# Another order of all operations in a gated recurrence with a highway layer

## The chip, the cores and the metric

The kernel runs on one core of a Trainium2 chip. The metric is the device time of one execution in microseconds (us). The core has five engines with an instruction queue each: TensorE (PE in the profile, its weight loads PEld), VectorE (DVE), ScalarE (ACT), GpSimd (POOL) and SyncE (SP), which here only issues the DMAs of the large tensors.

## The reference

The first stage is a gated linear recurrence over the tokens of four sequences, the second a highway layer on its result.

```python
# x, f_logit: (4, 6336, 256) float32; lower_bound: (256,)
sig = 1.0 / (1.0 + np.exp(-f_logit))
f = lower_bound + (1.0 - lower_bound) * sig
for t in range(6336):                       # h starts at 0 in each sequence
    h = f[:, t] * h + (1.0 - f[:, t]) * x[:, t]
    y[:, t] = h
# y as (25344, 256); w_h, w_t: (256, 256); b_t: (256,)
H = np.maximum(y @ w_h, 0.0)
T = 1.0 / (1.0 + np.exp(-(y @ w_t + b_t)))
out = T * H + (1.0 - T) * y
```

## The kernel before

The 25344 tokens are cut into 29 units: two of 2 blocks of 128 tokens, three of 4 blocks, 22 of 8 blocks (1024 tokens), one of 4 and one of 2. A unit goes through a fixed chain of operations, most of them once for each half (0 or 1) of the 256 channels:

| entry | engine | what it does |
|---|---|---|
| l, x | SP | load f_logit and x of the unit (up to 1 MB each) |
| u | ScalarE | sigmoid(-f_logit), both halves |
| b | GpSimd, or VectorE where marked v | product of u and x, one half |
| i | TensorE | transposes of u into PSUM, so that tokens lie along the free axis |
| f | ScalarE, or VectorE where marked v | the gate f from the transposed u |
| p | TensorE | transposes of b |
| s | VectorE | the scan: y = f * previous y + b along the tokens; it carries on from the unit before |
| z, g | TensorE | matmuls of y with w_t and with w_h |
| t | ScalarE | sigmoid of z |
| d | VectorE | the larger of g and a multiple of y, one half |
| e | GpSimd, or VectorE where marked v | product of d and t, cut into pieces of 256 to 2048 elements |
| o | TensorE | transposes d*t back and adds y, in PSUM |
| c | ScalarE, or VectorE where marked v | copies o to SBUF |
| w | SP | stores 4 blocks of the result (512 KB; single blocks in the last unit) |

An entry such as "e7.2v:1" names the operation, the unit (7), the half or piece (2), VectorE instead of the usual engine (v), and the buffer (1). The units 9 to 21 have one e for the whole unit (2048 elements); units 2 to 4 have two pieces, the other large ones three (1024, 512, 512). Besides these there are the entries of the start (dg, cb, cc, pc, pb, IW, WHa, WTa, wh, wt: constants and weights) and "k*n", n matmuls on zeros that only keep TensorE busy.

The order of the work is written out by hand as one string of 850 entries. A loop at the end takes the entries one by one and emits their instructions, and each engine's queue keeps that sequence (`pin`). So an instruction that has to wait also holds up all that follow it on its engine. The framework adds the waits for data and for the reuse of buffers: PSUM has two buffers a (one bank) for i and p, and three b (two banks) for z, g and o; SBUF has 6 of l and x, 4 of u and f, 8 of b and y, 5 of o.

Beside these waits there is one by hand. When GpSimd gets a product, it waits for the last VectorE product that stands ahead of it in the order, if no GpSimd product has waited for that one yet. There is no such wait in the other direction:

```python
    def shared(ins, gpsimd):
        if not gpsimd:
            held[:] = [ins]
        elif held:
            tc.add_manual_dep(ins.ins, held.pop().ins.name, ...)
```

The lines that the profile names: L268 is u, L276 b, L284 i, L293 and L295 f (VectorE, ScalarE), L304 p, L323 s, L335 and L115 z and g, L348 t, L352 d, L358 e, L380 and L381 o, L391 and L393 c (VectorE, ScalarE), L256 the loads, L397 the stores, L126 and L115 the matmuls on zeros.

Of the kernel before, what the change touches and what calls it, by code (L numbers as in the profile page):

```python
# [57 lines left out]
b6.0:5 f6.1:2 d4.0 k*3:1 p6.1:0 s6.1:4 i6.0:1 l8:2 u7:3 z5.1:1 g5.1:2 x8:2 b7.1:6 b7.0:7 f6.0:0 t4.0 t5.1:2 i7.1:1 p6.0:0
z5.0:0 f7.1:1 d5.1:2 t5.0 o3.0:1 g5.0:2 i7.0:1 c3.0:3 s6.0:5 e5.1v w1.0 l9:3 e4.0 x9:3 w0.0 e5.2v p7.1:0 l10:4 w2.0 d5.0 e5.0
g6.0:0 z6.1:1 z6.0:2 u8:0 f7.0:3 t6.1:1 i8.0:1 e4.1v b8.0:1 b8.1:0 s7.1:6 f8.0v:2 l11:5 w3.0 t6.0 x10:4 x11:5 u9:1 d6.0:0  # L60
i8.1:0 g6.1:1 p7.0:1 s7.0:7 o5.1:2 f8.1:0 c5.1:1 o5.0:0 i9.1:0 d6.1 e6.0 p8.1:1 c5.0:0 f9.1:1 e6.2 z7.0:2 t7.0:0 o4.0:0
p8.0:0 c4.0:2 u10:2 w5.1 b9.1:3 e6.1 l12:0 w4.0 l13:1 g7.1:1 s8.1:2 i9.0:1 g7.0:2 o6.0:0 s8.0:3 i10.1:0 f9.0:3 b9.0:2 x12:0
# [10 lines left out]
c11.0v:3 z13.1:0 f18.0:1 t13.1 g14.0:1 d14.0:1 i16.0:0 w11.0 b16.1:1 e13.0 p15.0:1 l20:2 f16.0:3 u17:2 z14.0:2 s15.0:6
o12.0:0 g14.1:1 i16.1:0 t14.0:2 b17.0:3 c12.0:0 x18:0 p15.1:1 o12.1:2 d14.1 s15.1:7 f16.1:0 w12.0 z14.1:1 c12.1:1 p16.0:0
i17.0:1 t14.1 g15.1:0 z15.0:2 w12.1 x19:1 s16.0:2 p16.1:0 f17.0:2 o13.0:1 d15.1:0 u19:3 t15.0:1 p17.0:1 o13.1:0 c13.0:2
c13.1:3 b17.1:2 e14.0 s16.1:3 z15.1:2 i17.1:0 g16.0:1 s17.0:0 g16.1:0 d16.0:2 t15.1 f17.1:3 x20:2 d16.1 u20:0 i18.1:1 z16.0:2
t16.0:0 p17.1:0 g15.0:1 z16.1:0 f18.1:0 w13.1 l21:4 b18.0:4 b18.1:5 t16.1 s17.1:1 w13.0 o14.0:2 d15.0 l22:3 i19.1:1 o14.1:0
c14.0:0 f19.1:2 z17.1:1 p18.0:0 e16.0v c14.1:1 b19.1:6 w14.0 b19.0:7 x21:3 e15.0v i19.0:1 t17.1:2 g17.0:2 z17.0:0 f19.0:3
o16.1:1 b20.0:0 s18.0:4 b20.1:1 t17.0 c16.1:3 p18.1:1 i20.0:0 f20.0:1 u21:2 d17.0:1 s18.1:5 g17.1:0 o16.0:2 d17.1 p19.1:0
w14.1 c16.0:2 z18.1:1 z18.0:0 p19.0:1 t18.1:0 e17.0 w16.1 o15.1:2 s19.1:2 l23:5 s19.0:3 x22:4 b21.0:3 i21.1:0 g18.1:1 t18.0  # L80
c15.1:0 g18.0:0 f21.1:0 d18.1:2 w15.1 u22:1 i20.1:1 f20.1:2 d18.0 b21.1:2 e18.0 p20.0:0 o15.0:2 z19.1:1 w16.0 o17.0:0 s20.0:6
p20.1:1 c15.0:1 b22.0:4 b22.1:5 g19.0:2 c17.0:3 t19.1:1 i21.0:0 f21.0:3 u23:3 x23:5 g19.1:0 s20.1:7 z20.0:1 p21.0:1 d19.0:0
t20.0:2 o17.1:2 w15.0 p21.1:0 d19.1 s21.0:0 o18.1:0 b23.1:6 s21.1:1 c17.1:0 z19.0:1 z20.1:2 i22.0:1 c18.1:2 t19.0 t20.1
g20.1:0 d20.1:1 f22.0:1 e19.0v l24:0 o18.0:1 w17.1 i22.1:0 g20.0:2 c18.0:1 f22.1:2 i23.1:1 z21.0:0 f23.1:3 d20.0 p22.0:0
o19.0:1 l28:1 x24:0 t21.0:0 w17.0 s22.0:4 p22.1:1 g21.1:2 o19.1:0 d21.1:2 s22.1:5 i23.0:0 c19.0:0 u24:0 f23.0:0 l25:2 w18.0
w19.0 z21.1:1 t21.1 b23.0:7 c19.1:3 g21.0:2 e20.0 i24.1:0 p23.1:1 d21.0 s23.1:2 z22.1:1 f24.1:1 b24.0:0 b24.1:1 e21.0 g22.0:0
z22.0:2 d22.0:0 p23.0:0 t22.1:1 u25:2 t22.0 w18.1 x25:1 w19.1 i24.0:1 o20.0:1 f24.0:2 c20.0:1 g22.1:0 s23.0:3 o20.1:2 i25.0:1
p24.0:0 d22.1 c20.1:0 o21.0:1 g23.0:0 u28:1 f25.0:3 e22.0 e22.1 e22.2 l26:4 c21.0:2 s24.0:6 d23.0:1 w20.0 z23.1:2 i28.1:1
p24.1:0 o21.1:1 f28.1:0 t23.1:2 s24.1:7 i28.0:1 c21.1:3 f28.0:2 g23.1:0 o22.0:2 x26:2 d23.1 u26:3 i25.1:1 b25.0:3 b25.1:2
e23.1 p25.0:0 c22.0:1 s25.0:0 f25.1:1 e23.2v z24.0:1 z24.1:0 g24.1:2 i26.1:0 p25.1:1 t24.0:0 f26.1:3 t24.1 d24.1:2 s25.1:1  # L90
z23.0:1 g24.0:2 w21.1 l27:3 i26.0:0 b26.0:4 b26.1:5 t23.0 o22.1:0 z25.1:1 p26.1:1 d24.0 e24.2v x27:3 u27:0 w22.0 w20.1 x28:4
g25.0:2 c22.1:3 e24.0 t25.1:1 b27.1:6 e24.1 e23.0v b27.0:7 b28.0:0 f26.0:1 s26.1:4 d25.0:0 w22.1 o23.1:0 z25.0:1 c23.1:1
# [345 lines left out]
```

## Time and profile before

| what | us |
|---|---|
| time, median of 3 runs | 206.16 (205.93 to 207.3) |
| span of the profiled execution | 204.7 |
| VectorE busy | 193.0 (162 instructions) |
| ScalarE busy | 193.1 (201) |
| TensorE busy | 191.6 (1826 matmuls) |
| GpSimd busy | 175.6 (98) |
| DMA | 78.68 MB, 384 GB/s over the span |

The profile gives one execution's span, from its first to its last instruction; it names no time of its own for that execution, which is therefore set beside the runs' median (1.46 more than the span). Busy time is the sum of an engine's instructions. A row of the timeline has the start, the time from there to the end of the last instruction of the row, engine and line, operation, output and inputs, shapes and count; in brackets stands the idle time ahead of it and what ended it. On an engine the next instruction mostly starts a little before the one ahead is reported as finished, so the time that an instruction takes up on its queue is read from one start to the next. A row that groups instructions has their count, then busy us and the mean ns of one, then the idle time before them.

### The profile page before, as it was taken

The page shows a single profiled execution, that of the slowest core. Times are in us where ns is not written, and L with a number is a line of the kernel's source. Part 1 is how long each engine was busy: PE and PEld are TensorE (multiplying, and loading weights), DVE is VectorE, ACT ScalarE, POOL GpSimd, SP SyncE. Part 2 cuts the span into 40 slices and gives each one's busy share as a digit, 9 for nine tenths or more (in the row PEclk, how much of TensorE's full clock was granted, in tenths as well). Part 3 has the DMA queues.
Part 4 walks back from the last instruction along what each step waited for, and adds up shares of the span by engine and source line. Part 5 has one row for each costly group of instructions (what it writes and reads, how often), then busy time and mean ns, then how long its engine had stood idle before and what let it go on. Part 6 is the DMA issues. An engine that isn't in the chain of part 4 may idle for free. (4 is left out here: it accounts for less than half of the span.)

```text
span 204.7 us, 4658 instructions
## 1 busy us (share of the span) xinstructions
PE 191.6 (94%) x1826; PEld 131.9 (64%) x1826; DVE 193.0 (94%) x162; ACT 193.1 (94%) x201; POOL 175.6 (86%) x98
## 2 busy tenths in 40 slices
...
GB/s 176 387 415 429 410 421 415 413 424 420 422 419 411 429 423 415 425 415 422 428 402 426 429 417 419 418 425 423 413 337 400 425 390 307 352 283 22 396 330 241
DMA packets 16413, 78.68 MB, mean 384 GB/s; under 512 B 1796, under 2 KB 2568, under 8 KB 10760
## 3 DMA queue, kind: packets, MB, share of 16 engines
...
q10 hardware_dynamic: 8, 0.00, 0.0%
...
## 5 line engine op out<-in xcount | busy, mean ns | idle before, releaser
L276 POOL TENSOR_TENSOR bv<-u,x 128x1024 bf16<-128x1024 f16 (+2 forms) x53 | 104.2, 1988 | 14.8 <-DVE d L358 5.7
L323 DVE TENSOR_TENSOR_SCAN y<-f,y,bT 128x1024 bf16<-128x1024 f16 (+5 forms) x56 | 106.9, 1925 | 0.2
L358 POOL TENSOR_TENSOR d<-d,t 128x512 bf16<-128x512 bf16 (+3 forms) x32 | 70.4, 2213 | 4.1 <-DVE d L358 1.8
L352 DVE SCALAR_TENSOR_TENSOR d<-y,ncc,g 128x1024 bf16<-128x1024 bf16 (+2 forms) x58 | 63.2, 1105 | 0.3 <-PE g L115 0.2
L348 ACT ACTIVATE t<-z,bt 128x1024 bf16<-128x1024 f32 (+2 forms) x58 | 62.4, 1112 | 0.8 <-PE z L115 0.8
L295 ACT ACTIVATE f<-uT,ncc 128x1024 f16<-128x1024 f16 (+2 forms) x55 | 60.8, 1120 | 0.8 <-DVE y L323 0.2
L393 ACT COPY o<-op 128x1024 f32<-128x1024 f32 (+2 forms) x53 | 52.8, 1036 | 1.9 <-ACT t L348 1.0
L268 ACT ACTIVATE u<-l 128x2048 f16<-128x2048 f32 (+2 forms) x29 | 51.5, 1776 | 2.5 <-DMA l<-in_f_logit_dram 2.5
L380 PE MATMUL op<-diag,y 128*128 128x128 f16 x396 | 49.7, 219 | 0.9 <-ACT t L348 0.4
L381 PE MATMUL op<-ident_b,d 128*128 128x128 bf16 x396 | 49.7, 219 | 0.8 <-POOL d L358 0.8
L381 PEld LDWEIGHTS <-d 128*128 128x128 bf16 x396 | 44.0, 113 | 4.8 <-POOL d L358 1.7
L380 PEld LDWEIGHTS <-y 128*128 128x128 bf16 x396 | 44.2, 113 | 2.3
L335 PE MATMUL z<-y,w_sb 128*128 128x512 bf16 (+1 forms) x116 | 40.0, 368 | 0.8 <-DVE d L352 0.3
L335 PE MATMUL g<-y,w_sb 128*128 128x512 bf16 (+1 forms) x116 | 40.3, 368 | 0.0
L304 PE MATMUL bT<-ident_f,bv 128*128 128x128 f32 x198 | 32.1, 278 | 2.9 <-DVE y L323 1.1
L115 PE MATMUL g<-y,w_sb 128*128 128x512 bf16 x88 | 33.3, 379 | 0.0
L115 PE MATMUL z<-y,w_sb 128*128 128x512 bf16 x88 | 33.3, 379 | 0.0
L284 PE MATMUL uT<-ident_h,u 128*128 128x128 f16 x396 | 31.4, 219 | 2.0 <-DVE y L323 1.1
L284 PEld LDWEIGHTS <-u 128*128 128x128 f16 x396 | 25.9, 98 | 11.1 <-issue 3.1
L335 PEld LDWEIGHTS <-w_sb 128*128 128x128 f16 x232 | 22.3, 98 | 15.7 <-ACT f L295 0.2
L304 PEld LDWEIGHTS bT<-ident_f,bv 128*128 128x128 f32 x198 | 22.1, 140 | 13.3 <-issue 4.7
L115 PEld LDWEIGHTS <-w_sb 128*128 128x128 f16 x176 | 17.2, 98 | 15.8 <-issue 1.7
...
## 6 DMA issues: line engine op xcount, KB each, us to landing
...
l<-in_f_logit_dram SPq DMA_DIRECT2D x22, 1024.0 KB, 14.0
...
```

What stands on the lines that cost most here:

```text
L115: return pe.add_instruction(mybir.InstMatmult(name=nc.get_next_instruction_name(), start_tensor_calc=start, stop_tensor_calc=stop, tile_si ...
L276: shared(pin(e.tensor_mul(bv[:, :nb // 2].rearrange("p k d j -> p k j d"), st[n]["u"][:, :nb, own].rearrange("p (k j) d -> p k j d", j=2), ...
L284: pin(nc.tensor.transpose(uT[:, j * P:(j + 1) * P], st[n]["u"][:, j, h * P:(h + 1) * P], ident_h))
L295: pin(nc.scalar.activation(to, of, AF.Identity, scale=ncc[:, h:h + 1], bias=1.0))
L304: pin(nc.tensor.transpose(words[:, k:k + g * (P - 1) + 1:g], pair, ident_f))
L323: pin(nc.vector.tensor_tensor_scan(y[:, c:e], st[n]["f", h][:, c:e], st[n]["bT", h][:, c:e], 0.0 if fresh else carry[h], op0=ALU.mult, op1 ...
L335: pin(nc.tensor.matmul(p[:, a:e], w, half(n, "y", ki)[:, a:e], start=ki == 0, stop=ki == NH - 1))
L348: pin(nc.scalar.activation(half(n, "t", m), st[n]["z", m][:, :tokens(n)], AF.Sigmoid, bias=bt[:, m:m + 1]))
L352: pin(nc.vector.scalar_tensor_tensor(half(n, "d", m), half(n, "y", m), ncc[:, m:m + 1], st[n]["g", m][:, :tokens(n)], op0=ALU.mult, op1=AL ...
L358: shared(pin(e.tensor_mul(st[n]["d"][:, a:c], st[n]["d"][:, a:c], st[n]["t"][:, a:c])), not eng)
L380: pin(nc.tensor.matmul(o, half(n, "y", h)[:, cols], diag[:, h], start=True, stop=False))
L381: pin(nc.tensor.matmul(o, half(n, "d", h)[:, cols], ident_b, start=False, stop=True))
```

## The change

Only the string of the order is changed: the same operations of the same units stand in another sequence, with other buffer numbers, and some go to another engine. On VectorE there are five f instead of three, 18 e instead of 22, two c instead of four, and the same number of b. The matmuls on zeros are 27 in both, at other places. The diff, cut to the start, the places around the VectorE products of units 3 to 11 and of 15 and 16, and the end:

```diff
     order = """
-k*3:a0 x0:0 pc:0 l0:0 l1:1 cc u0:0 k*3:1 pb:2 i0.0:1 k*4:0 dg wh u1:1 b0.1v:0 f0.0:0 b0.0v:1 i1.0:0 x1:1 l2:2 wt IW f1.0v:1 p0.0:1
-WHa cb i0.1:0 s0.0:0 f0.1:2 x2:2 b1.1v:2 b1.0v:3 k*2:0 i1.1:1 k*1:0 p0.1:0 f1.1:3 p1.0:1 s0.1:1 k*1:0 p1.1:0 l3:3 g0.0:0
-s1.0:2 g0.1:1 u2:2 s1.1:3 x3:3 k*1:2 i2.1:1 d0.1:0 l4:4 WTa d0.0 g1.0:2 i2.0:0 g1.1:1 z1.1:0 b2.1v:4 f2.1:0 d1.1:1 d1.0
-f2.0:2 p2.1:1 s2.1:4 b2.0:5 t1.1:0 z0.0:1 z0.1:0 z1.0:2 u3:3 x4:4 t0.1:1 t1.0 t0.0 l5:5 x5:5 p2.0:0 b3.1:6 i3.1:1 f3.1:1
-s2.0:5 e0.1v e0.0v e1.1v k*3:0 i3.0:0 g2.0:0 l6:0 u4:0 e1.0v x6:0 b3.0:7 z2.0:2 b4.0:1 f3.0:3 p3.1:1 t2.0:2 d2.0:2 g2.1:1
-i4.1:0 o0.0:0 z2.1:2 f4.1:0 s3.1:6 b4.1:0 d2.1 c0.0:0 t2.1 p3.0:1 i4.0:0 f4.0:2 s3.0:7 e2.1v k*3:1 p4.0:0 z3.1:1 u5:1 p4.1:1
...
-p9.1:1 u11:3 b10.0:4 b10.1:5 b11.0:6 d7.1:2 d7.0 e7.0 z8.1:1 g8.1:2 s9.1:0 f10.1:0 p9.0:0 t8.1:2 c6.0:3 d8.1:1 i11.1:1 s9.0:1
-o6.1:1 z7.1:0 f11.1:2 c6.1:1 i10.0:1 t7.1 g8.0:2 p10.0:0 z9.0:1 w6.0 w5.0 f10.0v:1 d8.0 u12:0 t9.0:1 z9.1:0 w6.1 e8.1v e7.2v
-t9.1 e7.1v l14:2 x13:1 i12.1:1 f12.1:3 z8.0:2 g9.0:1 o7.1:0 s10.0:4 b11.1:7 t8.0 i11.0:1 p10.1:0 l16:3 f11.0:1 o7.0:2 u13:1
...
-t11.1 x15:3 l18:5 u15:3 s12.0:3 g11.0:0 p13.1:1 o9.0:1 d11.0 i14.1:0 b13.0:2 z12.0:0 c9.1:2 s13.1:0 f14.1:3 c9.0:3 o10.1:2
-e11.0v x16:4 i15.1:0 p13.0:1 t12.0:1 o10.0:1 c10.1:0 f15.1:2 s13.0:1 b14.0:4 b14.1:5 c10.0:1 g12.1:0 g12.0:2 i14.0:0 w9.1
...
-t26.0 s27.1:3 p28.1:0 o25.0:1 s28.0:6 c25.0:3 o25.1:0 z27.1:a1 s28.1:7 g27.1:a0 d26.1 c25.1 e26.0 d27.1:2 t27.1:0 o25.3:1
-o25.2:0 c25.2:2 e26.2v c25.3 e26.1v g27.0:a1 z27.0:a0 o26.2:2 t27.0 d27.0 o26.3:0 c26.3:1 g28.0:a1 z28.0:a0 w23.0 t28.0:1
-c26.2v d28.0:0 o26.1:1 o26.0:2 w25.0 g28.1:a1 z28.1:a0 e27.1 c26.1v:0 w25.1 d28.1 c26.0 e27.0 t28.1 o27.1:0 e28.0 o27.0:1
-e28.1 w26.1 c27.1v:3 o28.0:2 c27.0 o28.1:a1 w26.0 c28.0:2 c28.1:4 w27.0 w28.0 w28.1
+k*3:0 x0:0 l0:0 u0:0 pb:1 i0.1:0 l1:1 pc:2 cc i0.0:1 wh f0.0:0 x1:1 f0.1:1 u1:1 b0.1v:0 b0.0v:1 dg p0.0:1 cb IW k*2:0 p0.1:0 s0.0:0
+i1.0:1 l2:2 s0.1:1 wt x2:2 WHa i1.1:0 b1.0v:2 b1.1v:3 f1.0:2 l3:3 u2:2 x3:3 g0.1:2 f1.1v:3 l4:4 p1.0:1 WTa s1.0:2 g0.0:1 p1.1:0 s1.1:3
+i2.1:1 i2.0:0 f2.1:0 x4:4 d0.0:0 k*1:0 b2.1v:4 d0.1 g1.1:1 z0.1:0 f2.0:1 t0.1:0 b2.0:5 p2.1:1 z0.0:2 p2.0:0 u3:3 d1.1:1 t0.0 s2.1:4
+z1.1:0 z1.0:1 s2.0:5 e0.1 t1.1:1 b3.1:6 i3.1:1 t1.0 e0.0v g1.0:2 d1.0 p3.1:0 f3.1:2 i3.0:1 u4:0 f3.0:3 l5:5 s3.1:6 z2.0:0 g2.1:1 b3.0:7
+t2.0:2 i4.1:1 e1.0 d2.1:2 x5:5 b4.0:1 l6:0 p3.0:0 z2.1:2 x6:0 b4.1:0 e1.1 o0.0:0 f4.1:0 l7:1 t2.1 c0.0:0 i4.0:1 g2.0:1 s3.0:7 p4.0:0
+z3.0:2 f4.0v:1 k*3:0 p4.1:1 s4.0:0 s4.1:1 u5:1 o1.0:0 e2.1 t3.0:0 d2.0 x7:1 b5.1:2 c1.0:1 i5.1:0 g3.0:2 f5.1:2 d3.0:0 l8:2 z4.0:0
+b5.0:3 e2.0 i5.0:1 g3.1:1 d3.1 z3.1:2 e3.0 p5.1:0 z4.1:1 s5.1:2 t4.0:1 f5.0:3 t3.1 g4.0:0 g4.1:2 p5.0:1 u6:2 t4.1 b6.1:4 i6.1:0 s5.0:3
+d4.0:1 d4.1 o2.0:1 f6.1:1 i6.0:0 e3.1v c2.0:2 f6.0:0 l9:3 p6.1:1 x8:2 g5.0:0 z5.1:1 b6.0:5 s6.1:4 d5.0:2 l10:4 z5.0:2 u7:3 b7.1:6 e4.0
+t5.1:2 p6.0:0 i7.1:1 x9:3 w1.0 t5.0 s6.0:5 f7.1:2 k*3:1 g5.1:0 b7.0:7 o3.0:1 i7.0:1 d5.1 p7.1:0 u8:0 c3.0:3 w2.0 f7.0:3 z6.1:2 e4.1
+e5.2 z6.0:0 i8.0:1 b8.0:1 e5.1 t6.0:0 e5.0v u9:1 s7.1:6 g6.0:1 f8.0v:1 d6.0:0 k*1:0 i8.1:0 b8.1:0 p7.0:1 l11:5 s7.0:7 o5.1:0 g6.1:1
+e6.0 t6.1 k*3:2 f8.1:0 d6.1 x10:4 u10:2 p8.0:0 c5.1:4 o5.0:2 b9.0:2 i9.1:1 o4.0:1 l12:0 s8.0:2 f9.1:2 g7.1:0 d7.1:2 c4.0:1 i9.0:1
+b9.1:3 c5.0:2 p8.1:0 z7.1:1 z7.0:0 f9.0:3 x11:5 g7.0:2 i10.1:1 b10.0:4 l13:1 t7.1:1 t7.0 f10.1:1 e6.2 b10.1:5 s8.1:3 u11:3 w3.0 w5.0
+w0.0 p9.0:0 z8.0:1 e6.1 t8.0:2 b11.1:6 b11.0:7 d7.0 w4.0 z8.1:0 e7.2v k*3:2 i10.0:1 k*4:2 g8.1:2 e7.1 u12:0 s9.0:0 k*3:a0 f10.0v:0
+e7.0v t8.1 p9.1:1 i11.1:0 d8.1:1 f11.1:3 u13:1 o6.1:1 g8.0:2 s9.1:1 d8.0 e8.0 e8.2 o6.0:0 c6.0:3 p10.0:0 i11.0:1 o7.1:2 x12:0 g9.0:0
...
+s11.1:7 x14:2 f13.1:2 i13.0:0 d10.1:2 t10.1:1 c8.0:1 p12.1:1 z10.0:2 f13.0:1 w6.1 t10.0 g11.1:0 w8.1 g10.0:1 s12.1:2 u14:3 x15:3
+i12.0:0 g11.0:2 d11.1:1 z11.0:0 d10.0 l18:4 d11.0 e10.0 p12.0:1 f12.0:3 z11.1:1 o9.1:2 t11.0:2 o9.0:0 b15.1:4 s12.0:3 t11.1 c9.1:0
+i14.1:0 c9.0:3 b14.0:7 p13.1:1 z12.1:1 f14.1:0 z12.0:2 b14.1:5 g12.1:0 t12.1:0 t12.0 i15.1:0 b15.0:6 f15.1:3 e11.0v w9.1 u18:0 w7.1
...
+i19.1:1 z16.1:2 t16.0:2 t16.1 o14.1:0 s17.1:1 f19.1:1 g15.0:1 x20:2 c14.1:0 i19.0:0 o14.0:2 e16.0v f19.0:3 w14.1 d15.0 p18.0:1 z17.1:0
+l21:3 i18.1:0 b19.1:6 g17.1:1 c14.0:1 s18.0:4 f18.1:0 o16.0:2 w11.0 t17.1:1 d17.1:1 b19.0:4 c16.0:4 e15.0v p18.1:1 i20.0:0 s18.1:6
...
+o23.0:2 o24.1:1 f27.1:1 e24.1 c23.0:0 i27.0:1 g25.1:0 c24.1:4 w22.1 o24.0:2 f27.0:2 e25.0v c24.0:1 p27.0:0 w23.1 z26.1:1 d25.1 b28.0:0
+b27.1:3 p28.0:1 z26.0:0 g26.0:2 s27.0:2 e25.1v w24.1 s28.0:3 d26.0:1 o25.1:a0 t26.1:1 p27.1:1 o25.0:1 w21.1 s27.1:5 w24.0 t26.0 g26.1:0
+e25.2 o25.3:2 w23.0 d26.1 c25.1:3 c25.0 c25.3:4 o25.2:a0 z27.1:1 e26.0 p28.1:1 c25.2 e26.2v t27.1:2 s28.1:7 z27.0:2 g27.1:a0 t27.0
+o26.3:0 d27.1:2 w25.0 e26.1 o26.2:1 g27.0:2 z28.0:a1 c26.3:2 o26.1:0 c26.2 t28.0:0 o26.0:1 w25.1 w26.1 z28.1:a0 g28.1:a1 e27.1v d27.0
+e27.0v o27.0:2 c26.1:1 d28.1:0 c26.0 t28.1 o27.1:0 w26.0 c27.0v:0 g28.0:1 c27.1 w27.0 e28.1 d28.0 e28.0v o28.1:a1 o28.0:a0 c28.1:3
+w28.1 c28.0:4 w28.0
 """
```

More of the change, by code (lines that the diff above doesn't have):

```diff
@@ L58 @@
[L58 to L62, printed above, removed]
@@ L73 @@
[L73 to L77, printed above, removed]
@@ L78 @@
[L78 to L92, printed above, removed]
```

30 lines of the change are left out of this document (21 added, 9 removed).

## The prediction

> **What bounds the kernel now.** I read the page's busy line first, then the stages, then single rows.
>
> ```profile
> PE 191.6 (94%) x1826; PEld 131.9 (64%) x1826; DVE 193.0 (94%) x162; ACT 193.1 (94%) x201; POOL 175.6 (86%) x98
> ```
>
> Three engines are busy 94% of the span, so shares decide nothing. The stages say more (busy us of PE, PEld, DVE, ACT, POOL; then clock, DMA share, GB/s):
>
> ```profile
> 0.00:10.00 10.00, 8.24 (x33) 3.08 (x34) 4.50 (x14) 5.93 (x11) 2.49 (x13) 1.00 0.77 278
> 30.00:86.00 56.00, 53.08 (x520) 37.34 (x520) 56.00 (x42) 56.00 (x51) 52.91 (x25) 1.00 1.02 420
> 180.00:190.00 10.00, 10.00 (x106) 7.49 (x106) 9.83 (x9) 8.91 (x10) 9.53 (x8) 1.00 0.39 155
> 196.00:204.70 8.70, 3.82 (x58) 3.41 (x55) 3.13 (x6) 3.70 (x8) 3.21 (x4) 0.90 0.71 275
> ```
>
> From 30 to 86 us VectorE and ScalarE are never idle; only the first 10 us and the last 9 hold slack. To see which engine sets the end I count VectorE's work by start-to-start steps, since the next instruction starts about 0.08 us before the one ahead is reported done:
>
> ```profile
> 164.54 1.25 DVE L352 SCALAR_TENSOR_TENSOR d<-y,ncc,g 128x1024 bf16<-128x1024 bf16 x1
> 165.71 2.33 DVE L323 TENSOR_TENSOR_SCAN y<-f,y,bT 128x1024 bf16<-128x1024 f16 x1
> 167.97 1.24 DVE L352 SCALAR_TENSOR_TENSOR d<-y,ncc,g 128x1024 bf16<-128x1024 bf16 x1
> ```
>
> So d takes 1.17 us and a scan 2.26. Counted in the old order with such steps, 187.4 us of VectorE work are left from s1.0 on, 111.6 from e11.0v on, and 5.8 after the last scan s28.1:
>
> ```profile
> 9.53 1.36 DVE L323 TENSOR_TENSOR_SCAN y<-f,y,bT 128x256 bf16<-128x256 f16 x2
> 85.81 1.20 DVE L358 TENSOR_TENSOR d<-d,t 128x2048 bf16<-128x2048 bf16 x1
> 190.42 2.55 DVE L323 TENSOR_TENSOR_SCAN y<-f,y,bT 128x512 bf16<-128x512 f16 x3
> 200.82 0.73 SPq L397 DMA_DIRECT2D out_dram<-o  x1
> ```
>
> Start plus work left is 9.53 + 187.4 = 196.9, then 85.81 + 111.6 = 197.4, then (190.42 + 2.55) + 5.8 = 198.8. I call this sum **VectorE's due end**. Over 180 us it grows by 1.9: VectorE hardly ever waits and bounds the kernel. The span ends at 204.7, about 6.0 after the due end: TensorE trails VectorE, the last store is issued at 200.82, and 3.9 us more go by until the span's end. ScalarE has slack only at the end, and loads are early (ScalarE waits 2.5 us for them in all).
>
> GpSimd is the fourth bound, and it decides here:
>
> ```profile
> 51.38 8.52 POOL L276 TENSOR_TENSOR bv<-u,x 128x1024 bf16<-128x1024 f16 x4
> 59.85 2.13 POOL L358 TENSOR_TENSOR d<-d,t 128x1024 bf16<-128x1024 bf16 x1
> 79.46 4.09 POOL L358 TENSOR_TENSOR d<-d,t 128x2048 bf16<-128x2048 bf16 x1
> 83.52 2.15 POOL L276 TENSOR_TENSOR bv<-u,x 128x1024 bf16<-128x1024 f16 x1
> 50.26 1.16 POOL L358 TENSOR_TENSOR d<-d,t 128x512 bf16<-128x512 bf16 x1
> 87.09 4.25 POOL L276 TENSOR_TENSOR bv<-u,x 128x1024 bf16<-128x1024 f16 x2 [1.43 <-DVE d L358]
> ```
>
> Start to start, a product b of 1024 takes (59.85 - 51.38)/4 = 2.12 us, an e of 2048 takes 4.06, an e of 512 takes 1.12, and one of 1024 about 2.12 too. Note how b13.0 ends at 85.67, just ahead of VectorE's product e11.0v at 85.81. Where the two engines' products do meet, one waits:
>
> ```profile
> 145.51 4.29 POOL L276 TENSOR_TENSOR bv<-u,x 128x1024 bf16<-128x1024 f16 x2
> 149.09 1.78 DVE L358 TENSOR_TENSOR d<-d,t 128x2048 bf16<-128x2048 bf16 x1
> 120.43 2.35 DVE L358 TENSOR_TENSOR d<-d,t 128x2048 bf16<-128x2048 bf16 x2
> 121.78 3.01 POOL L276 TENSOR_TENSOR bv<-u,x 128x1024 bf16<-128x1024 f16 x1 [1.44 <-DVE d L358]
> ```
>
> e19.0v starts at 149.09 while GpSimd runs until 149.80, and lasts 1.78 instead of the 1.20 of e11.0v: VectorE lost 0.57 of the 0.71 that GpSimd had left. In the last two rows VectorE was first, and GpSimd's product took 3.01 instead of 2.15.
>
> **The change, part by part.** The same 850 entries come in a new order. Nothing is added but engine choices, and no transfer changes size.
>
> *VectorE's work.* Two products of 256 and five of 512 leave VectorE, three of 1024 come to it; two f more (one of 512, one of 256); two copies of 512 fewer.
>
> ```profile
> L358 DVE TENSOR_TENSOR d<-d,t 128x512 bf16<-128x512 bf16 x13 | 5.1, 424 | 0.1
> L358 DVE TENSOR_TENSOR d<-d,t 128x1024 bf16<-128x1024 bf16 x1 | 0.7, 678 | 0.0
> L358 DVE TENSOR_TENSOR d<-d,t 128x256 bf16<-128x256 bf16 x4 | 0.9, 282 | 0.0
> L293 DVE TENSOR_SCALAR f<-uT,ncc 128x256 f16<-128x256 f16 x1 | 0.5, 483 | 1.4 <-PE uT L284 1.4
> L391 DVE COPY o<-op 128x512 f32<-128x512 f32 x3 | 2.1, 691 | 0.4 <-PE op L381 0.2
> ```
>
> With 0.08 taken off each: products -2x0.20 - 5x0.35 + 3x0.60 = -0.35; f +0.40 +0.65 (between the 256 and 1.18 for 1024) = +1.05; copies -2x0.61 = -1.22. Sum **-0.5**. ScalarE loses two f and gains two copies, about 0; GpSimd gains about 0.5.
>
> *The start.* Before, ScalarE idles until the second load, and VectorE waits 1.37 for uT:
>
> ```profile
> 4.14 0.63 ACT L268 ACTIVATE u<-l 128x512 f16<-128x512 f32 x1 [1.29 <-DMA l<-in_f_logit_dram]
> 5.96 0.63 ACT L268 ACTIVATE u<-l 128x512 f16<-128x512 f32 x1 [1.19 <-DMA l<-in_f_logit_dram]
> 6.97 0.48 DVE L293 TENSOR_SCALAR f<-uT,ncc 128x256 f16<-128x256 f16 x1 [1.37 <-PE uT L284]
> 21.84 2.15 POOL L276 TENSOR_TENSOR bv<-u,x 128x1024 bf16<-128x1024 f16 x1 [2.14 <-ACT u L268]
> ```
>
> The loads go out in the same sequence. Now f0.0 and f0.1 lie in ScalarE's 1.19 of idle time, so s0.0 and s0.1 come first. cc now waits for i0.1, thus for u0 (4.77), so it comes about 1 us later, hidden by the wait for uT. Adding rows, s1.0 starts near 9.1 and not 9.53: **-0.5** (0 if u2's load is no earlier, -0.9 at best). More products of units 0 to 2 go to GpSimd and fill the 2.14 that it idled before b5.1 (last row); b2.0 starts near 11.5 behind b2.1v, and adding up its queue from there gives b5.1 finished near 22.95 and b6.1 near 29.5, with VectorE there at 23.2 and 29.4 and a transpose of some 0.6 between: two waits of 0.4, against 0.5 of waits before in that stretch: **+0.3**.
>
> *The middle, 30 to 86 us.* This is the largest term. GpSimd's b6.0 waits for e3.1v (the shared() helper); from there on GpSimd has no wait that the order enforces until b19.1. Up to the end of e10.0 it has 15 b of 1024, nine e of 512, two of 1024 and two of 2048: 31.8 + 10.1 + 4.2 + 8.1 = 54.2 us. VectorE has, from the end of e3.1v to e11.0v, 14 scans, 14 d, two f and three products: 31.6 + 16.4 + 2.3 + 1.6 = **51.9 us**. VectorE's four products e5.0v, e7.2v, e7.0v and e11.0v therefore each meet a GpSimd product in progress. Walking both queues from e3.1v's end (29.85), with VectorE's wait ending 0.14 before GpSimd's product (0.71 - 0.57) and GpSimd's next one then waiting in turn: VectorE's due end is then 196.7 (9.1 + 186.8 left at s1.0, + 0.8 of waits), and each product comes at the due end less the work left from it on. e5.0v (159.8 left) comes at 36.9, b7.0 ends at 29.95 + 7.5: wait 0.4. e7.2v (144.3 left) comes at 52.8; b10.0 ends 16.1 + 0.6 later, at 54.1: 1.2. e7.0v (140.5) comes at 57.8; e7.2v, then e6.2, b10.1 and e6.1 end at 58.8: 0.9. e11.0v (114.7) comes at 84.5; e7.0v and 26.4 of GpSimd's queue end at 85.8 with e10.0: 1.1. Sum 3.6, less the 0.1 that e8.1v cost before: **+3.5**. From below this is 0, if GpSimd is ahead of my count; from above it is the whole next product at each of the four, since no row shows VectorE waiting between two products that GpSimd has back to back: another 1.1 to 2.1 each, +6. I take 3.5, the value by the e19.0v row, since it is the nearest there is. Behind a waiting product stand scans (s7.1, s9.0, s13.1), and TensorE, then ScalarE, wait for them; nothing hides it, as VectorE has no slack.
>
> The Trainium skill, page "SBUF — State Buffer", section "Who interferes with whom", says that a VectorE instruction with two SBUF inputs contends with a GpSimd instruction that reads SBUF, and that whoever issues first holds the port pair for its whole instruction while the other fully blocks. The trace agrees in kind (0.57 of the 0.71 left). By the rule alone each of the four waits would be the full rest, 0.14 longer, and the time 208.5; it does not say who goes next between back-to-back products.
>
> The four rows of GpSimd can be read by the reported length instead of the spacing:
>
> ```profile
> L276 POOL TENSOR_TENSOR bv<-u,x 128x1024 bf16<-128x1024 f16 x44 | 94.8, 2178 | 8.5 <-DVE d L358 5.7 <-ACT u L268 2.1 <-issue 0.4
> ```
>
> With 2.18 for each of the 15 b instead of 2.12, GpSimd's sum would be 0.9 longer and the waits with it. I keep the spacing, because 8.47 us from the first of four to the next instruction is what the queue really took. The Trainium skill, page "Perfetto Trace Analysis", section "GPSIMD Engine Instruction", likewise calls a GpSimd instruction's reported span unreliable and asks for the spacing of consecutive starts.
>
> *After e11.0v.* GpSimd's stretches between its holds fit: from e11.0v's end to e16.0v it has 33.4 us against VectorE's 34.2. e19.0v's 0.57 goes, and with VectorE late, ScalarE and TensorE have slack, so of the 1.4 that the due end grew here I keep 0.5 to 0.8: **-0.7**. The stores lag the loads more (36 stores instead of 39 ahead of the last load on SP's queue), and copies find their buffers free by bytes over 420 GB/s with some 2.7 us to spare (2.3 before): 0.
>
> *The tail.* Work after s28.1 falls from 5.8 to 3.65, since d26.1, e26.2v and two copies now lie ahead of it or on ScalarE. Its chain is d27.1, e27.1v, d27.0, e27.0v (2.05), o27.0 (0.65), c27.0v, d28.0, e28.0v (1.3), two o (0.5), c28.1 and c28.0 (0.7), w28.0 (0.2), then as long as from the last issue now (200.82) to 204.7 (3.9): 9.3, or 5.7 behind the due end instead of 6.0: **-0.3**.
>
> Sum: -0.5 - 0.5 + 0.3 + 3.5 - 0.7 - 0.3 = **+1.8**, so a span of 206.5. The three runs have a median of 206.16, 1.46 over the profiled span of 204.7; with the same 1.46 the time is 208.0.
>
> **Rivals.**
>
> *GpSimd keeps up*: if the middle's term is 0, the sum is -1.7, at 204.5. For it: b13.0 and e11.0v miss each other by 0.14 before. Against: 54.2 over 51.9 needs no fine reading. ScalarE then decides:
>
> ```profile
> 78.77 1.32 ACT L295 ACTIVATE f<-uT,ncc 128x1024 f16<-128x1024 f16 x1
> 80.11 2.35 DVE L323 TENSOR_TENSOR_SCAN y<-f,y,bT 128x1024 bf16<-128x1024 f16 x1
> ```
>
> f12.0 ends at 80.09 and s12.0 starts at 80.11, just in time. ScalarE has as much work ahead of f12.0 as before and is perhaps 0.4 earlier by the start; VectorE would be 1.1 earlier there: it waits 0.7, and the time is **205.2**. It goes below -1% only if the start brings its best 0.9 and ScalarE with it.
>
> *VectorE gets no turn between back-to-back GpSimd products*: slower on one mechanism, at e5.0v, e7.2v and e11.0v, deciding as soon as one waits past one boundary. Two waits more of 1.1 to 2.1 give **211**; all four with several boundaries, 214.
>
> *TensorE as the bound*: it is 10.00 of 10 busy at 180 to 190, and its chain ends the profile.
>
> ```profile
> 144.67 0.22 PE z L335
> 144.88 0.22 PE z L115
> ```
>
> A matmul of 512 columns takes 0.215 by these starts. Ten of the 27 filler matmuls ("k" entries) now stand around e7.2v. If their 2.2 us delay TensorE there instead of lying in its waits, the -1.7 becomes +0.5 without the collisions: **206.7**. Against: it has the same operations left from p26.0 on.
>
> **How the numbers follow.** About 1%, 2.06 us, is what a measurement of this kernel can tell from no change, so 204.1 and 208.2 are the bounds. The collisions as summed: 0.55, their own range 206.7 to 209.3, of it 0.30 within 1% and 0.25 slower. GpSimd keeps up: 0.25, of it 0.10 faster, 0.15 within 1%. No turn: 0.12, all slower. TensorE: 0.08, of it 0.05 within and 0.03 slower. So faster 0.10, same 0.50, slower 0.40. The range 205.0 to 211.0 leaves out a tenth at each end.
>
> **What would show it.** In the changed profile VectorE's products of 1024 and 2048 between 36 and 87 us should last 0.4 to 1.1 longer than 0.68 and 1.20, GpSimd be busy nearly without a gap from 30 to 86 us, TensorE idle more at 50 to 60 us, s1.0 start near 9.1, and the last scan end near 197 with 9.3 behind it. Plain 0.68 and 1.20 there would prove the main term wrong.

## The result: slower, and the profile after

The new order takes 211.8 us (median of four runs, 210.67 to 213.21) beside 206.2 for the old one: a ratio of 1.027 (1.021 to 1.032). Forecast were 208.0 and at most 211.0. The profiled execution took 210.67 itself, the least of the four, with a span of 208.9: 4.2 over the old span, where the sum said 1.8. So 2.4 of the 3.8 us that the forecast missed lie in this trace; the rest is the distance from this span to the median (2.9, taken as 1.46), which a trace can't show. Some executions of the kernels below were disturbed and took longer; their medians and ratios leave these out. Lines in the profile after are 3 lower (L355 is e, L273 b, L320 s, L265 u, L253 the loads, L394 the stores).

First the page's busy line and the same stages as before:

```profile
PE 191.5 (92%) x1798; PEld 134.1 (64%) x1826; DVE 196.0 (94%) x158; ACT 194.4 (93%) x201; POOL 176.7 (85%) x102
```
```profile
0.00:10.00 10.00, 6.50 (x26) 2.88 (x27) 4.62 (x15) 5.97 (x11) 2.48 (x13) 0.89 0.82 288
30.00:86.00 56.00, 53.10 (x491) 36.69 (x500) 56.00 (x39) 54.63 (x49) 54.61 (x29) 1.00 0.99 397
180.00:190.00 10.00, 9.95 (x112) 7.53 (x112) 10.00 (x9) 10.00 (x12) 8.49 (x6) 1.00 0.57 228
200.00:208.90 8.90, 4.45 (x60) 3.54 (x57) 4.29 (x9) 4.22 (x10) 1.48 (x2) 1.00 0.66 255
```

VectorE's busy time grew by 3.0 though its work fell by 0.5, so its instructions became longer. ScalarE, never idle from 30 to 86 us before, now idles 1.4 there; and the last column fell from 420 to 397 GB/s, which the prediction did not look for. The timeline shows the four products and the GpSimd products beside them:

```profile
38.11 1.33 DVE L355 TENSOR_TENSOR d<-d,t 128x1024 bf16<-128x1024 bf16 x1
54.35 1.25 DVE L355 TENSOR_TENSOR d<-d,t 128x512 bf16<-128x512 bf16 x1
59.01 1.38 DVE L355 TENSOR_TENSOR d<-d,t 128x1024 bf16<-128x1024 bf16 x1
85.58 2.14 DVE L355 TENSOR_TENSOR d<-d,t 128x2048 bf16<-128x2048 bf16 x1
36.73 2.16 POOL L273 TENSOR_TENSOR bv<-u,x 128x1024 bf16<-128x1024 f16 x1
38.84 2.73 POOL L355 TENSOR_TENSOR d<-d,t 128x512 bf16<-128x512 bf16 x2
82.56 4.08 POOL L355 TENSOR_TENSOR d<-d,t 128x2048 bf16<-128x2048 bf16 x1
```

e5.0v starts at 38.11, while b7.0 runs until 38.89, and lasts 1.33 instead of 0.68. GpSimd's next pair then takes 2.73 instead of some 2.3, as its first product waits in turn. e11.0v (85.58) waits for e10.0, which ends at 86.64. Counted from one start to the next, the four cost VectorE 0.67, 0.82, 0.71 and 0.94: **3.1 us** (the expectations below say 3.0).

The rest of the loss is not on VectorE's own rows. The stages behind 60 us, of after and then of before, with GB/s as the last column:

```profile
60.00:90.00 30.00, 28.19 (x278) 19.99 (x279) 30.00 (x20) 29.09 (x28) 29.74 (x14) 1.00 0.97 374
90.00:120.00 30.00, 28.16 (x276) 20.27 (x281) 29.86 (x21) 28.51 (x26) 28.03 (x11) 1.00 1.01 397
120.00:150.00 30.00, 28.64 (x278) 20.26 (x281) 28.77 (x19) 29.11 (x28) 25.00 (x11) 1.00 0.98 382
```
```profile
60.00:90.00 30.00, 28.91 (x295) 20.71 (x293) 30.00 (x21) 30.00 (x28) 26.86 (x12) 1.00 1.02 421
90.00:120.00 30.00, 29.04 (x272) 19.76 (x270) 29.88 (x21) 30.00 (x28) 30.00 (x12) 1.00 1.01 419
120.00:150.00 30.00, 29.48 (x301) 21.40 (x301) 30.00 (x21) 30.00 (x30) 28.35 (x12) 1.00 1.02 417
```

Before, the DMA ran at 417 to 421 GB/s in all three; at 421 its 78.68 MB alone take 187 us of the 204.7. After, (421 - 374) + (419 - 397) + (417 - 382) GB/s over 30 us each are 3.1 MB or 7.4 us of transfer that came later. SyncE's rows of after, and one of ScalarE, show why:

```profile
75.93 0.46 SPq L253 DMA_DIRECT2D l<-in_f_logit_dram  x1
85.68 1.62 SPq L394 DMA_DIRECT2D out_dram<-o  x3
...
112.85 0.34 SPq L253 DMA_DIRECT2D x<-in_x_dram  x1
124.92 0.33 SPq L394 DMA_DIRECT2D out_dram<-o  x1
125.30 0.42 SPq L253 DMA_DIRECT2D l<-in_f_logit_dram  x1
...
132.54 1.92 ACT L265 ACTIVATE u<-l 128x2048 f16<-128x2048 f32 x1 [0.89 <-DMA l<-in_f_logit_dram]
```

SyncE issues in order. From 75.93 to 85.68 it stands at the store w9.1 and from 112.85 to 124.92 at w14.1, until their copies are done; loads stand behind them. So l21 goes out at 125.30, and u21 on ScalarE waits for it until 132.54. In the view of waits (total us, times, longest) the longest one of a store for its copy is 10.8 us in after and was 6.6 in before. In total such waits are no longer than they were; what is new is how long single ones last:

```profile
SPq L394 <- ACT o L390: 105.5, 31, 10.8
```
```profile
SPq L397 <- ACT o L393: 107.0, 37, 6.6
```

### The profile page after: what moved, and what is told of

Its sections match the earlier page's. It is cut to its first block, busy times and chain, and to the rows that moved or that the text cites. A ratio compares the mean times of both kernels' runs of the same rounds, so it can differ in the third digit from the quotient of the medians.

```text
span 208.9 us, 4624 instructions
## 1 busy us (share of the span) xinstructions
PE 191.5 (92%) x1798; PEld 134.1 (64%) x1826; DVE 196.0 (94%) x158; ACT 194.4 (93%) x201; POOL 176.7 (85%) x102
## 2 busy tenths in 40 slices
DMA packets 16413, 78.68 MB, mean 377 GB/s; under 512 B 1796, under 2 KB 2568, under 8 KB 10760
## 4 chain that ended last, share of the span: by engine, by line
PE 34%; DVE 24%; POOL 13%; issue 12%; ACT 4%; DMA 3%; ACTq 0%; SPq 0%; POOLq 0%; DVEq 0%
DVE y L320 12%; POOL bv L273 8%; POOL d L355 6%; DVE d L349 6%; PE op L378 5%; PE g L332 5%; PE op L377 5%; PE bT L301 4%; PE z L332 4%; DVE d L355 4%; PE uT L281 4%; DMA l<-in_f_logit_dram 3%; PE z L112 3%; PE g L112 3%; DVE f L290 1%
## 5 line engine op out<-in xcount | busy, mean ns | idle before, releaser
L273 POOL TENSOR_TENSOR bv<-u,x 128x1024 bf16<-128x1024 f16 (+2 forms) x53 | 104.7, 1996 | 12.1 <-DVE d L355 5.2
L320 DVE TENSOR_TENSOR_SCAN y<-f,y,bT 128x1024 bf16<-128x1024 f16 (+5 forms) x56 | 107.3, 1926 | 1.7 <-ACT t L345 0.4
L355 POOL TENSOR_TENSOR d<-d,t 128x512 bf16<-128x512 bf16 (+3 forms) x36 | 71.3, 1990 | 9.9 <-ACT t L345 6.7
L345 ACT ACTIVATE t<-z,bt 128x1024 bf16<-128x1024 f32 (+2 forms) x58 | 57.0, 1012 | 1.0 <-PE z L332 0.6
L292 ACT ACTIVATE f<-uT,ncc 128x1024 f16<-128x1024 f16 (+2 forms) x53 | 54.6, 1036 | 1.9 <-PE uT L281 0.9
L390 ACT COPY o<-op 128x1024 f32<-128x1024 f32 (+2 forms) x55 | 49.6, 931 | 4.4 <-PE op L378 3.1
L265 ACT ACTIVATE u<-l 128x2048 f16<-128x2048 f32 (+2 forms) x29 | 48.7, 1680 | 2.4 <-DMA l<-in_f_logit_dram 2.4
L332 PE MATMUL z<-y,w_sb 128*128 128x512 bf16 (+1 forms) x114 | 40.5, 378 | 1.2 <-ACT t L345 0.7
L281 PEld LDWEIGHTS <-u 128*128 128x128 f16 x396 | 26.4, 99 | 12.1 <-issue 3.7
L332 PEld LDWEIGHTS <-w_sb 128*128 128x128 f16 x232 | 23.1, 101 | 16.7 <-issue 0.7
L112 PE MATMUL z<-y,w_sb 128*128 128x512 bf16 x82 | 31.1, 379 | 0.1
L301 PEld LDWEIGHTS bT<-ident_f,bv 128*128 128x128 f32 x198 | 22.5, 143 | 11.3 <-POOL bv L273 3.7
L112 PEld LDWEIGHTS <-w_sb 128*128 128x128 f16 x176 | 17.2, 98 | 17.2 <-issue 3.3
L112 PE MATMUL g<-y,w_sb 128*128 128x512 bf16 x72 | 27.3, 379 | 0.1
## 6 DMA issues: line engine op xcount, KB each, us to landing
x<-in_x_dram SPq DMA_DIRECT2D x22, 1024.0 KB, 12.2
```

Of the source, the lines that this page charges most:

```text
L112: return pe.add_instruction(mybir.InstMatmult(name=nc.get_next_instruction_name(), start_tensor_calc=start, stop_tensor_calc=stop, tile_si ...
L273: shared(pin(e.tensor_mul(bv[:, :nb // 2].rearrange("p k d j -> p k j d"), st[n]["u"][:, :nb, own].rearrange("p (k j) d -> p k j d", j=2), ...
L281: pin(nc.tensor.transpose(uT[:, j * P:(j + 1) * P], st[n]["u"][:, j, h * P:(h + 1) * P], ident_h))
L292: pin(nc.scalar.activation(to, of, AF.Identity, scale=ncc[:, h:h + 1], bias=1.0))
L301: pin(nc.tensor.transpose(words[:, k:k + g * (P - 1) + 1:g], pair, ident_f))
L320: pin(nc.vector.tensor_tensor_scan(y[:, c:e], st[n]["f", h][:, c:e], st[n]["bT", h][:, c:e], 0.0 if fresh else carry[h], op0=ALU.mult, op1 ...
```

## The experiments

Times beside which they stand: before was 206.5 to 206.7 in every set (206.2 beside after). Of a_nohold and a_sp2 one execution each remained, so these have a single time and no ratio.

**Where it is: stretches of the two orders joined.** h_start has the first 165 entries of after and then what is left in the sequence of before; h_end has before's first 400 and then the rest as in after; h_mid takes after between the two.

```diff
 h_start: -... l8:2 u7:3 z5.1:1 g5.1:2 b7.1:6 ...           (before, around entry 165)
          +... g5.0:0 z5.1:1 b6.0:5 s6.1:4 d5.0:2 | u7:3 g5.1:2 b7.1:6 ...
 h_end:   -... l17:0 p14.0:1 d12.0 c10.0:2 x16:4 ...        (after, around entry 400)
          +... d12.0 l17:0 g13.0:1 g13.1:0 z12.1:2 | b15.1:6 t12.1 b15.0:7 u18:0 ...
```

> The first 165 entries of the new order (to about 30 us), then the old order for all that is left. Theory (collisions of VectorE's and GpSimd's products between 36 and 87 us make the new order slow): only the new start is here, which left VectorE's due end 0.5 us later at s5.1 than the old one; 206.0 to 207.2. Rival (the new order is slow in all its parts, by waits of ScalarE, TensorE and the loads): 207.5 to 208.5.

> The first 165 entries of the old order, then the new order up to its 400th entry (about 30 to 90 us, with e5.0v, e7.2v, e7.0v and e11.0v as the new order places them), then the old order; without the new order's filler matmuls. Theory: VectorE waits some 3.0 us behind GpSimd's products here, so 208.5 to 210.5, and these four products last 1.2 to 2.1 us each. Rival: under 207.5.

> The first 400 entries of the old order (to about 90 us), then the new order. Theory: the new order's end is no worse by itself, the 2.4 us that it lost after e11.0v followed from the collisions ahead: 205.3 to 206.8. Rival: 208 to 209.

Measured: h_start 212.1 (1.025, 1.021 to 1.030), h_mid 220.8 (1.068, 1.064 to 1.072), h_end 217.0 (1.051, 1.045 to 1.056). None of the three lies where an expectation for its stretch could hold, because the join itself costs more than the stretch that it was to show: the rows of h_start, then h_end, have waits of 3 and 6 us at places where neither order has one.

```profile
78.96 1.11 ACT L346 ACTIVATE t<-z,bt 128x1024 bf16<-128x1024 f32 x1 [3.06 <-POOL d L356]
```
```profile
98.06 2.35 DVE L322 TENSOR_TENSOR_SCAN y<-f,y,bT 128x1024 bf16<-128x1024 f16 x1 [6.37 <-ACT f L294]
```

These three locate nothing by their times. Of use is only the start of h_start: VectorE's due end there is 198.3 at s5.1 against 197.4 in before, and 197.9 in after, so after's start costs 0.5 to 0.9 us.

**The collisions taken away.** a_memset is after with the four products as VectorE memsets (0.27 to 0.91 us, together 0.8 shorter than undisturbed products):

```diff
     def do_e(n, k, eng, slot):
         a, c = units[n][2][k:k + 2]
+        if eng and n in (5, 7, 11):
+            shared(pin(nc.vector.memset(st[n]["d"][:, a:c], 0.0)), False)
+            return
```

> The new order, but VectorE's products e5.0v, e7.2v, e7.0v and e11.0v are memsets of the same pieces, which read nothing (so parts of units 5, 7 and 11 of the output lack the gated term). They take nearly as long by themselves. Theory: the 3.0 us of waits go, and some of what followed from them: 207.0 to 209.0. Rival: 211 or more.

Measured: 211.9 (1.023, 1.017 to 1.028), in the rival's range. All four waits are gone and VectorE's due end at s13.1 is 198.4 instead of 201.1, yet the time gains nothing that stands clear of the noise. What took it is in two rows:

```profile
132.94 1.91 ACT L265 ACTIVATE u<-l 128x2048 f16<-128x2048 f32 x1 [3.13 <-DMA l<-in_f_logit_dram]
139.86 2.47 DVE L349 SCALAR_TENSOR_TENSOR d<-y,ncc,g 128x1024 bf16<-128x1024 bf16 x2 [3.76 <-PE g L112]
```

u21 comes at 132.94, as late as in after (132.54), but now has waited 3.13, not 0.89. A second bound lies under the first. From here the theory was two bounds, each hiding the other.

**The price of a collision, and of the holds.** b_nohold and a_nohold are before and after without the wait of GpSimd:

```diff
-        elif held:
+        elif False:
```

> The kernel before with no GpSimd instruction held by a VectorE product (the dependency that keeps GpSimd from starting beside it is left out; data dependencies stay). In the trace of before eight such holds made GpSimd wait 0.6 to 1.4 us. Theory (a VectorE product that finds a GpSimd product in progress waits for its end, and for the next too where GpSimd has one ready): VectorE loses 1 to 2 us at each of some of these places and GpSimd's lead takes little of it back: 209 to 216, with single VectorE products of 1024 or 2048 lasting 2 to 5 us. Rival (holding costs as much as it saves, a collision is a delay of the order of 0.5 us): 205.5 to 207.5.

> The kernel after with the same dependency left out: its six holds of 0.6 to 1.5 us go. The four products that already met a GpSimd one stay as they are. Theory: more VectorE products wait, each 1 to 2 us: 213 to 219. Rival (collisions are cheap, GpSimd's turn matters more; after lacks GpSimd time): 209.5 to 211.5.

Measured: b_nohold 217.8 to 220.1 (1.059, 1.052 to 1.066), above the range of its theory; a_nohold 217.1, once, within its own. In b_nohold eight VectorE products run into a GpSimd one, and from each start to the next VectorE's due end grows by 0.6 to 2.2, by 12.2 in all (e19.0v's 0.6 of before is among them); the profiled span grew by 11.3, from 204.7 to 216.0. Two of them:

```profile
22.24 4.27 POOL L276 TENSOR_TENSOR bv<-u,x 128x1024 bf16<-128x1024 f16 x2 [3.12 <-ACT u L268]
24.42 2.36 DVE L358 TENSOR_TENSOR d<-d,t 128x512 bf16<-128x512 bf16 x1
...
153.82 4.26 POOL L276 TENSOR_TENSOR bv<-u,x 128x1024 bf16<-128x1024 f16 x2
156.51 2.65 DVE L358 TENSOR_TENSOR d<-d,t 128x2048 bf16<-128x2048 bf16 x1
```

e3.1v takes 2.36 instead of 0.42 and ends 0.3 behind the GpSimd pair (1.94 lost of the 2.09 left); e19.0v loses 1.45 of the 1.57 that GpSimd had left. The Trainium skill, page "SBUF — State Buffer", section "Who interferes with whom", has it that the engine that issues first keeps the shared ports for its whole instruction; these two agree to within 0.15 us, and so do five of the other six. The eighth, e8.1v, let a whole further product go first (last section).

**SyncE's order made anew.** a_sp moves each store to where its copy ended and lets no load stand behind a waiting store; am_sp has the memsets too:

```diff
-... w8.1 x15 l18 w9.1 w7.1 w9.0 l16 l17 x16 w10.0 x17 w10.1 w8.0 w5.1 l19 ... x19 w12.1 x20 w14.1 l21 ...
+... x14 x15 w8.1 l18 l16 w8.0 w9.1 w9.0 l17 x16 x17 w10.1 w10.0 l19 ... w13.1 w12.1 x20 l21 w13.0 w14.1 ...
```

> The kernel after with SyncE's stores and loads in another order and nothing else moved: from 45 us on each store stands where its copy ended in the run of after, and no load stands behind a store that still waits for its copy (l21, which went out at 125.3 behind w14.1, now goes out near 114). Theory of two bounds (four VectorE products that met a GpSimd one cost VectorE 3.0 us by 83 us; late loads hold ScalarE to nearly the same time at 132.5): VectorE's loss stays and only what comes behind s13.1 goes, 1 to 2.5 of it: 209.3 to 211. Rival A, the late loads are the whole loss and the collisions are hidden: 206 to 208. Rival B, the loads have no part in it and idle time behind 110 us has another cause: 211 to 212.5.

> Both at once: SyncE's order as in a_sp, and e5.0v, e7.2v, e7.0v and e11.0v as VectorE memsets (leaves out the gated term in parts of units 5, 7 and 11), so that none of the four meets a GpSimd product. Theory of two bounds: with both gone VectorE is due 198.4 at 85 us as it was in a_memset, and no wait for l21 gives it back: 206 to 208.3. Rival A (late loads alone): the same as a_sp within 0.7. Rival B (another cause behind 110 us): 210.5 to 212, as a_memset was.

Measured: a_sp 213.7 (1.034, 1.030 to 1.038), am_sp 212.7 (1.028, 1.024 to 1.032): not faster than after, and outside the expectations of the theory and of its rivals. In am_sp no u waits for l21 any more, but c7.1 now waits for the store of its output buffer:

```profile
67.17 1.94 ACT L394 COPY o<-op 128x1024 f32<-128x1024 f32 x2 [1.91 <-DMA out_dram<-o]
```

a_sp2 and am_sp2 have an order sought by a rate of 419 GB/s, so that loads and output buffers both keep 1.5 us to spare, and other output buffers:

```diff
+... w8.1 x14 w5.1 l18 w8.0 x16 w6.1 w7.1 l16 l17 x17 w10.1 w9.1 w9.0 l19 w11.0 l20 l21 w12.0 x18 ...
```

> The kernel after with SyncE's order made anew and its output buffers handed out anew (in a_sp and am_sp the loads came in time, but a copy, c7.1, waited 1.9 us for its output buffer, whose store had gone out behind three loads). The new order was sought so that by the rate of before (419 GB/s) each load lands 1.5 us ahead of its first use and each store ahead of the next copy into its buffer. Theory of two bounds, collisions and SyncE's queue, each hiding the other: only a little goes, 209 to 211. Rival A (the queue is the whole loss): 206 to 208. Rival B (neither; the order of the computing instructions themselves is longer behind 60 us): 211 to 213.

> SyncE's order and output buffers as in a_sp2, and the four colliding products as VectorE memsets (leaves out the gated term in parts of units 5, 7 and 11). Theory of two bounds: no wait of ScalarE for a load or for an output buffer above 0.5 us between 50 and 180, VectorE due near 198.5 to 200 to the end, time 206 to 208.5. Rival A: equal to a_sp2 within 0.7. Rival B: 210 to 212.5 as a_memset and am_sp were, with VectorE's idle time of 3 us or more between 60 and 150 still there and its releaser TensorE or ScalarE with no wait for the DMA behind it.

Measured: a_sp2 219.2, once, am_sp2 215.6 (1.040, 1.035 to 1.045), both above every expectation. Another load was late, l23 in am_sp2:

```profile
142.41 1.91 ACT L266 ACTIVATE u<-l 128x2048 f16<-128x2048 f32 x1 [4.62 <-DMA l<-in_f_logit_dram]
```

The orders of these four moved the wait instead of removing it (so the rows of am_sp and am_sp2), and could not tell the theory from a rival by which the computing entries' own order is longer.

**Bytes taken away, nothing moved.** Each store of four blocks writes only the first:

```diff
-        pin(nc.sync.dma_start(rows(out, n, j0, j1), st[n]["o", j0][:, :j1 - j0]))
+        pin(nc.sync.dma_start(rows(out, n, j0, j1)[:, :1], st[n]["o", j0][:, :1]))
```

> The kernel after, each store of four row blocks writing only the first of them (leaves three quarters of most of the output unwritten; every instruction and wait stays, about 19 of 78 MB of DMA go). Theory of two bounds: loads land sooner, the wait of u21 at 132 and what follows from it go, VectorE's four collisions (3.0 us) stay: 208.5 to 210.5. Rival A (loads are the whole loss): 205.5 to 207.5. Rival B (the DMA has no part in it; the order of the computing instructions is longer by itself): 211 to 212.5.

> Light stores as in a_light and the four colliding products as VectorE memsets (leaves out the gated term in parts of units 5, 7 and 11 too). Theory of two bounds: both are gone, 205.5 to 208. Rival A: as a_light within 0.7. Rival B: 210 to 212.5, as a_memset.

> The kernel before with the same light stores. Its trace shows nearly no wait of a computing engine for a load or a store: within 1 us of before (205.5 to 207) by the theory of two bounds, and by Rival B too. Should it gain 2 us or more, before stands on the DMA as well and the light stores say less on what the change did.

**One load moved.** l21 alone goes ahead of w14.1:

```diff
-... x20:2 c14.1:0 i19.0:0 o14.0:2 e16.0v f19.0:3 w14.1 d15.0 p18.0:1 z17.1:0 l21:3 i18.1:0 ...
+... x20:2 l21:3 c14.1:0 i19.0:0 o14.0:2 e16.0v f19.0:3 w14.1 d15.0 p18.0:1 z17.1:0 i18.1:0 ...
```

> The kernel after with one load, l21, moved ahead of the store w14.1 in SyncE's order (it goes out near 113.5 in place of 125.3). Theory of two bounds, with l21 as the transfer that decides: the 0.9 us wait of u21 goes, the four collisions stay, and the end comes 0 to 2 earlier: 209.5 to 211.5. Rival C (the lateness is spread over all loads behind 100 us, the next one takes the place of l21): 211 to 212.5.

> The same move with the four colliding products as VectorE memsets (leaves out the gated term in parts of units 5, 7 and 11). Theory with l21: the 3.1 us wait of u21 and VectorE's 3.8 us behind it go: 207.5 to 209.5. Rival C: another load or an output buffer waits in its place, 210.5 to 212.5.

Measured, with the ratio to before:

| | collisions as they are | the four as memsets |
|---|---|---|
| after's transfers | 211.8: 1.027 (1.021 to 1.032) | 211.9: 1.023 (1.017 to 1.028) |
| l21 moved | 211.3: 1.024 (1.021 to 1.027) | 209.2: 1.012 (1.010 to 1.015) |
| light stores | 208.8: 1.011 (1.008 to 1.015) | 206.6: 1.000 (0.997 to 1.002) |

b_light: 205.5, 0.995 (0.993 to 0.997).

All five fell where the theory of two bounds had them, b_light just at the lower edge; a_l21 also lies in its rival's range. Taking the collisions away is worth nothing clear of the noise beside late transfers, 2.1 with l21 moved and 2.2 with light stores. Lighter transfers are worth 3.0 beside the collisions and 5.3 without (by the ratios 3.2 and 4.8, as the rows of the table were not taken in one set). In a_light the four collisions are there to within 0.03:

```profile
38.66 1.35 DVE L355 TENSOR_TENSOR d<-d,t 128x1024 bf16<-128x1024 bf16 x1
54.92 1.25 DVE L355 TENSOR_TENSOR d<-d,t 128x512 bf16<-128x512 bf16 x1
59.58 1.39 DVE L355 TENSOR_TENSOR d<-d,t 128x1024 bf16<-128x1024 bf16 x1
86.15 2.17 DVE L355 TENSOR_TENSOR d<-d,t 128x2048 bf16<-128x2048 bf16 x1
```

while behind them VectorE's due end grows by only 0.5, from 201.7 at s13.1 to 202.2 at s28.1; in after it grew by 2.6 there. Down the table, this growth is 2.6, 2.2 and 0.5 with the collisions and 7.1, 3.9 and 1.1 with the memsets: what the memsets save ahead of s13.1 is lost behind it for as long as the transfers are late.

In a_l21 nothing clear is gained, and the trace shows what Rival C had: u21 no longer waits, but c16.1 just ahead of it does, for the output buffer that w14.1 empties, the very store that l21 went ahead of. So u21 starts at 132.41, hardly sooner than in after (132.54).

```profile
131.50 1.01 ACT L391 COPY o<-op 128x1024 f32<-128x1024 f32 x1 [0.77 <-DMA out_dram<-o]
```

In am_l21 l21 goes out at 111.32 and u21 starts at 129.69 without a wait:

```profile
111.32 0.34 SPq L254 DMA_DIRECT2D l<-in_f_logit_dram  x1
...
129.69 1.91 ACT L266 ACTIVATE u<-l 128x2048 f16<-128x2048 f32 x1
```

So this one load gave back what the collisions would have gained (2.7 by the medians, 2.2 by the ratios). Another 2.6 us (209.2 against 206.6) hang on the other transfers: in am_l21 ScalarE still waits 0.6, 0.2 and 0.8 for output buffers (c11.1, c12.1, c16.1) and 0.7 for a load (u25). What each of these costs stays open.

The 1.0 that b_light gains is not of this kind. VectorE's due end grows no less in its middle than in before (from e11.0v on 1.3 and 1.4). In its trace the span is 1.3 shorter: 0.6 is gained in the start, before any store has gone out, 0.3 is lost behind it, and 1.0 is gained from the due end at s28.1 to the span's end (4.9 instead of 5.9), where the last stores are lighter. In after that last piece is 5.2 with and without light stores.

By the two traces the 4.2 us between the spans of after and before are +0.5 up to s5.1, +3.2 from there to s13.1, where the collisions stand, +1.2 behind s13.1 and -0.7 at the end. These say where, not what each cause costs: beside late transfers the collisions cost the time nothing clear, and without late transfers 1.4 to 2.2 (the memsets are 0.8 shorter than the products that they replace). am_light is still 1.1 above b_light, and VectorE's due end in its trace is later by as much (1.0) already at s5.1, so most of that belongs to the start.

## Why the prediction was wrong

*The middle, +3.5*: right on VectorE's rows. The four products that it named each met a GpSimd product; it said 0.4, 1.2, 0.9 and 1.1, measured are 0.67, 0.82, 0.71 and 0.94. GpSimd was busy 54.61 of 56 us. That VectorE waits one product and then gets its turn, the e19.0v row's reading, held at all four and at seven of the eight in b_nohold. As a term to be added up it failed: without these waits (a_memset) the time stayed at 211.9, since late transfers took their place.

*The start, -0.5, and the waits behind it, +0.3*: too low by 1.2, the second miss. s1.0 came at 9.25 (9.1 was said), but the due end was 197.9 at s5.1 and not 196.7:

```profile
9.25 1.39 DVE L320 TENSOR_TENSOR_SCAN y<-f,y,bT 128x256 bf16<-128x256 f16 x2 [0.20 <-PE bT L301]
13.09 2.45 DVE L320 TENSOR_TENSOR_SCAN y<-f,y,bT 128x512 bf16<-128x512 f16 x2 [0.44 <-ACT t L345]
25.11 4.58 DVE L320 TENSOR_TENSOR_SCAN y<-f,y,bT 128x1024 bf16<-128x1024 f16 x2 [0.29 <-ACT f L292]
```

s2.1 and s5.1 wait for ScalarE here, which the sum followed only up to s1.0. The granted TensorE clock was 0.89 in the first 10 us of this execution, but that isn't the cause: h_start has the same start at a clock of 1.00 there and is due at 198.3 by s5.1, no sooner.

*After e11.0v, -0.7*: this step failed. It kept 0.5 to 0.8 of growth and got 2.6, 1.9 too little. Its words on the transfers, "copies find their buffers free by bytes over 420 GB/s ... 0", tested the output buffers alone and took the 420 for granted; the loads were put aside as early at the outset. In after SyncE stands 9.8 and 12.1 us, from one issue to the next, at stores whose copies come late, the DMA falls to 374 to 397 GB/s, and the loads behind arrive when they are needed or later. The output buffers did not come out at 0 either: c13.1 waits 0.70 for one (its store, w8.0, stands behind w10.1 in the order), ScalarE has 0.17 of idle time from there to t16.1, and e16.0v on VectorE waits 0.72 for t16.1:

```profile
109.24 1.01 ACT L390 COPY o<-op 128x1024 f32<-128x1024 f32 x1 [0.70 <-DMA out_dram<-o]
123.02 1.23 DVE L355 TENSOR_TENSOR d<-d,t 128x2048 bf16<-128x2048 bf16 x1 [0.72 <-ACT t L345]
```

With light stores (a_light) neither u21 nor a copy waits for the DMA there, the step gives the 0.5 that it forecast, and the time is 208.8. Light stores leave SyncE's order as it is (its longest stand at a store is 12.1 there) and take bytes away, so they show that the transfers are the cause, but not that their order is; for the order there is only l21's move, and that only beside the memsets.

*The tail, -0.3*: right in kind; it gained more. After the last scan come 8.7 us, where 9.3 were forecast:

```profile
199.48 0.74 DVE L320 TENSOR_TENSOR_SCAN y<-f,y,bT 128x256 bf16<-128x256 f16 x1
```

*The rivals*: "GpSimd keeps up" and "TensorE as the bound" did not come. "No turn" had a time near the result (211), but that is luck: in after every one of the four got its turn. The rival that did come, late loads as a second bound, was missing. Having VectorE busiest was no proof that it alone bounds: the Trainium skill, page "Perfetto Trace Analysis", section "Identifying the Most-Contended Engine", would optimize the engine of the highest occupancy first (the DMA it judges by its bandwidth); here a_memset shortened the way of that engine by 2.7 us up to s13.1, and the time did not move clear of the noise.
